# Output blocks of the end in the load buffers, and their stores as single 128-row transfers

## The chip, the cores and the metric

The kernel runs on one core of a Trainium2 chip. The time is the device time of one execution in microseconds (us). A core has TensorE (PE, matrix products into PSUM), VectorE (DVE), ScalarE (ACT), GpSimd (POOL) and SyncE (SP, which in this kernel only issues transfers), and 16 DMA engines that move data between the core's on-chip memory and DRAM. A transfer is issued by an instruction on SP or ACT; each of the two has its own DMA queue (q1 is SP's, q10 is ACT's in the profile).

## The reference

Eight batches of sigmoid attention with 12 heads, 448 tokens and a head dimension of 64, then a mixing layer over the tokens:

```python
scores = q @ k.T / sqrt(64) - log(448)
x = concat_heads(sigmoid(scores) @ v)          # 8 x 448 x 768
W_tok = (x @ w_q) @ (x @ w_k).T / sqrt(64)     # 448 x 448 per batch
out = relu(W_tok @ x) @ w_out                  # 8 x 448 x 768, float32
```

The output is 8 x 448 rows of 768 floats, 11 MB in all. A row is 3072 bytes.

## The kernel before, in words

All instructions are emitted in an order written out by hand: the string `PLAN` (L126) holds one letter per step, and the loop at L801 emits each. `S` and `P` are attention steps, `W`, `N`, `U`, `M` those of the mixing layer, and `O`/`o`/`I`/`i` a part of the last product (`relu(...) @ w_out`); a small letter puts its PSUM copy on ACT, a capital one on DVE. The string ends `...IxiiNIIuiIMiImmIIIOooOOOOoOOoooooo`.

The tokens of a batch are numbered `t = 7 p + i` with p of 0..63 and i of 0..6. Two batches form a pair `w`; its 14 values of (batch, i) are taken two at a time, in seven chunks `m` = 0..6. A chunk is 128 output rows: 64 tokens of one i on partitions 0 to 63 and 64 tokens of the next on partitions 64 to 127, each with 768 columns, computed as two halves of 384 columns (`nb` 0 and 1). The output of a chunk is 384 KB. Rows of one i lie 7 x 3072 bytes apart in DRAM; rows of i and i+1 of the same p are neighbours.

The last pair (w = 3) is what the change touches. Its chunks 0 to 2 are computed by `out_halves` (L535): for each of the two i values, two groups of 64-row products, an ACT or DVE copy (L557), and a DVE addition (L558); then two stores of 64 x 2 x 384 floats on SP (L567). Its chunks 3 to 6 are computed by `out_chunk` (L576) after everything else: 12 matmuls a chunk at L595, a copy out of PSUM per half (L624), and the function `store` (L600). In chunk 6 the second half is cut in two again, DVE copies one piece (L621) and ACT the other (L622), and each half of 384 columns is stored by itself. `store` issues one transfer for each 64 partitions: the first on SP, the second on ACT where `tail` is true, which it is for chunks 3 to 6 of the last pair (the attention is done by then).

The finished block lies in a tile `o`. These come from a pool of three buffers (`p_o`, L60), taken in turn, for all output of the kernel; a buffer can be written again once the stores that read it have landed. The inputs come through six other buffers of 128 x 896 floats (`lds`, L103), also taken in turn, by `ld_next` (L106). The last load is issued at 138.8 us of the span. The set `cast` holds all loads that have been converted; it has `len(ORDER) + 2` members when none is outstanding.

Of the kernel before, what the change touches and what calls it, by code (L numbers as in the profile page):

```python
# [9 lines left out]
F32 = mybir.dt.float32  # L10
# [7 lines left out]
def kernel(  # L18
# [12 lines left out]
    nc = tc.nc  # L31
    B, H, S, HD = q.shape
    D = H * HD
    DH = moe_w_q.shape[1]
    assert DH == HD == 64 and S == 448 and D == 768
    P = 128
    NI, NP = 7, 64
    NU = B
    NJ = H // 4
    NC = D // P  # L40
    NB = D // 2
# [6 lines left out]
    def pool(name, bufs, **kw):  # L48
        return ctx.enter_context(tc.tile_pool(name=name, bufs=bufs, **kw))
# [10 lines left out]
    p_o = pool("o", 3)  # L60
# [10 lines left out]
    def bank2():  # L71
        n = free2.pop(0)
        return n, pairs[n], pairs16[n]

    def bank1():
        if halves:
            n, b = halves.pop(0)
        else:
            n, b = free2.pop(0), 0
            halves.append((n, 1))  # L80
        return (n, b), pairs[n][:, b], pairs16[n][:, b]

    def release(fb):
        if isinstance(fb, int):
            free2.append(fb)
        elif (fb[0], 1 - fb[1]) in halves:
            halves.remove((fb[0], 1 - fb[1]))
            free2.append(fb[0])
        else:
            halves.append(fb)  # L90
# [15 lines left out]
    def ld_next():  # L106
        nld[0] += 1
        return lds[(nld[0] - 1) % 6]
# [386 lines left out]
    ot = {}  # L495
# [39 lines left out]
    def out_halves(act):  # L535

        if opened:
            w, m, part, fb, ps = opened.pop()
        else:
            w, m, nb = chunks.pop(0)  # L540
            assert nb < 0
            part = 0
            ot[0] = p_o.tile([P, 2, NB], F32, tag="o", name="o")
        o = ot[0]
        b, h = divmod(part, 2)
        if not h:
            fb, ps, _ = bank2()
        for c in range(3 * h, 3 * h + 3):
            t0 = 2 * S * c + m * P + b * NP
            for y in range(2):  # L550
                for x in range(2):
                    nc.tensor.matmul(  # L552
                        ps[HALF[x], y, 0:NB], mxs[w][HALF[y], t0 : t0 + NP], wout16[HALF[y], c, x * NB : (x + 1) * NB],
                        start=(c == 0), stop=(c == NC - 1),
                    )
        if h:
            COPY["s" if act else "v"](out=o[:, b], in_=ps[:, 0, 0:NB])  # L557
            nc.vector.tensor_tensor(out=o[:, b], in0=ps[:, 1, 0:NB], in1=o[:, b], op=ALU.add)  # L558
            release(fb)
        if part < 3:  # L560
            opened.append((w, m, part + 1, fb, ps))
            return
        (b0, i0), (b1, i1) = divmod(2 * m, NI), divmod(2 * m + 1, NI)
        for x in range(2):
            cols = slice(x * NB, (x + 1) * NB)
            if b0 == b1:
                nc.sync.dma_start(  # L567
                    out=out[2 * w + b0].rearrange("(p i) d -> p i d", i=NI)[:, i0 : i1 + 1, cols], in_=o[HALF[x]],
                )
                continue  # L570
            for y, (b, i) in enumerate(((b0, i0), (b1, i1))):
                nc.sync.dma_start(
                    out=out[2 * w + b].rearrange("(p i) d -> p i d", i=NI)[:, i, cols], in_=o[HALF[x], y],
                )

    def out_chunk(act, tail):  # L576

        if opened:
            w, m, nb, fb, ps = opened.pop()
            part = 1  # L580
        else:
            w, m, nb = chunks.pop(0)
            if nb < 0:
                nb = 0
                chunks.insert(0, (w, m, 1))
            fb, ps, _ = bank2() if w == NU // 2 - 1 and not chunks else bank1()
            part = 0
        last = isinstance(fb, int)
        if nb == 0 and not part:
            ot[0] = p_o.tile([P, D], F32, tag="o", name="o")  # L590
        o = ot[0]

        def block(ps, w0, w1, c0, c1):
            for c in range(c0, c1):
                nc.tensor.matmul(  # L595
                    ps, mxs[w][:, 2 * S * c + m * P : 2 * S * c + (m + 1) * P],
                    wout16[:, c, w0:w1], start=(c == 0), stop=(c == NC - 1),
                )

        def store(cols):  # L600
            for y in range(2):
                b, i = divmod(2 * m + y, NI)
                eng = nc.scalar if tail and y else nc.sync
                eng.dma_start(
                    out=out[2 * w + b].rearrange("(p i) d -> p i d", i=NI)[:, i, cols],
                    in_=o[HALF[y], cols],
                )

        ps = ps if last or part else ps[:, 0:NB]
        if last:  # L610
            for c in range(part * NC // 2, (part + 1) * NC // 2):
                for x in range(2):
                    block(ps[:, x, 0 : NB // 2], NB + x * NB // 2, NB + (x + 1) * NB // 2, c, c + 1)
        else:
            block(ps, nb * NB, (nb + 1) * NB, part * NC // 2, (part + 1) * NC // 2)
        if not part:
            opened.append((w, m, nb, fb, ps))
            return
        if last:
            h = NB // 2  # L620
            nc.vector.tensor_copy(out=o[:, NB : NB + h], in_=ps[:, 0, 0:h])  # L621
            nc.scalar.copy(out=o[:, NB + h :], in_=ps[:, 1, 0:h])  # L622
        else:
            COPY["s" if act else "v"](out=o[:, nb * NB : (nb + 1) * NB], in_=ps)  # L624
        release(fb)
        split = tail and w == NU // 2 - 1 and m == NI - 1
        if nb or split:
            store(slice(nb * NB, (nb + 1) * NB) if split else slice(0, D))
# [23 lines left out]
    def cols(r):  # L652
        return slice(r.start * HD, r.stop * HD)
# [8 lines left out]
        out=ident, in_=ident, compare_op=ALU.not_equal, fill=1.0, base=0,  # L662
# [8 lines left out]
    for t in wqks:  # L671
# [3 lines left out]
    ORDER = (  # L675
# [5 lines left out]
    )  # L681
# [7 lines left out]
    ORDER = [(x[0], int(x[1:])) for x in ORDER.replace(".", "").lower().split()]  # L689
# [3 lines left out]
    used, loaded, cast = set(), set(), set()  # L693
# [72 lines left out]
    for t16, t32, r, e in (  # L766
# [3 lines left out]
            out=t16[:, r].rearrange("p i b d -> p b i d"),  # L770
            in_=t32[:, :, cols(r)].rearrange("p b (i d) -> p b i d", d=HD),
# [3 lines left out]
    def tr_part(nm, t16, r, e):  # L775
# [13 lines left out]
        out=k016[:, K3].rearrange("p i b d -> p b i d"), in_=k0[:, :, cols(K3)].rearrange("p b (i d) -> p b i d", d=HD),  # L789
# [11 lines left out]
    for t in PLAN:  # L801
# [6 lines left out]
        tail = done["S"] == N * NI  # L808
# [3 lines left out]
        elif kind == "P":  # L812
            n, i = divmod(c, NI)
# [25 lines left out]
        elif kind == "x":  # L839
            tr_x(c, tail, t in "XY", "s" if t in "yY" else "v")  # L840
        elif kind == "W":
            mlp_wqk(*divmod(c, NC), tail, t in "wl", t in "Ll")
        elif kind == "C":
            for y in range(2):
                nc.sync.dma_start(out=wout16[HALF[y], NC + c, :], in_=wout16[HALF[1 - y], c, :])
        elif kind == "N":
            mlp_wkn(c)
        elif kind == "U":
            (mlp_tmp_tiled if t in "Tt" else mlp_tmp)(c, t in "ut")
        elif kind == "M":  # L850
            u, x = divmod(c, NC // 2)
            mlp_mix(u, x, t == "m", tail)
            if x == NC // 2 - 1:
                if u // 2 in TW:
                    chunks.extend((u // 2, ((u % 2, i), (u % 2, 6 - i))) for i in range(3))
                    if u % 2:
                        chunks.append((u // 2, ((0, 3), (1, 3))))
                else:
                    chunks.extend((u // 2, m, -1) for m in (range(3, NI) if u % 2 else range(3)))
        elif kind == "O":  # L860
            if (opened or chunks)[0][0] in TW:
                out_pair(t == "o")
            elif t in "Ii":
                out_halves(t == "i")
            else:
                out_chunk(t == "o", tail)
# [29 lines left out]
```

## Time and profile before

| | us |
|---|---|
| median of 3 runs | 189.16 (188.65 to 190.88) |
| the profiled execution, its own time | 189.54 |
| its span, first to last instruction | 187.8 |
| PE busy | 176.3 (94%) |
| ACT busy | 163.6 (87%) |
| DVE busy | 140.8 (75%) |
| POOL busy | 106.7 (57%) |
| granted clock of PE | 0.999 |

The profile is of one execution, so its span is 1.74 us shorter than the same execution's own time, and that time is 0.38 us over the median. The span is followed by PE nearly from end to end; the shares of busy time say little on the last 10 us, in which PE ends its work and only copies and stores remain. This stretch is read from the timeline, the waits and the DMA view.

### The profile page before, as it was taken

To read this page: it belongs to the slowest core of one execution; us is meant where nothing else is said; L and a number is where in the kernel's file an instruction comes from. 1 tells how busy PE (TensorE), PEld (TensorE's weight loads), DVE (VectorE), ACT (ScalarE), POOL (GpSimd) and SP (SyncE) were. 2 spreads that over 40 slices of the span, in tenths; PEclk is the share of its full clock that TensorE was granted. 3 is DMA by queue.
4 is the path that set the end of the run, shared out by engine and by line. 5 is a ranking of instruction groups with operands and counts; after the bars stand their busy time and mean duration, and the time that the engine had idled before them with its cause. 6 is when DMAs were issued, how large, how long until landed. Compare 5 with 4: busy or idle time off the path is not lost.

```text
span 187.8 us, 8516 instructions
## 1 busy us (share of the span) xinstructions
PE 176.3 (94%) x3648; PEld 115.8 (62%) x3648; DVE 140.8 (75%) x216; ACT 163.6 (87%) x210; POOL 106.7 (57%) x145
## 2 busy tenths in 40 slices
PE   7898899989999999999999999999999999999990
PEld 7343456544555454565555776667998889776650
DVE  3534697677868999999898999888768565787810
ACT  4699999999999989999999999898999989975130
POOL 1457796972959989899899767495032910010000
PEclk9999999999999999999999999999999999999999
DMA  5999999954699989999988999993998733603485
GB/s 175 364 388 377 333 381 393 362 171 139 204 335 402 404 254 292 383 289 310 271 237 262 335 336 353 287 296 101 247 339 282 184 92 87 165 13 85 101 237 168
DMA packets 26389, 48.97 MB, mean 261 GB/s; under 512 B 4080, under 2 KB 20208, under 8 KB 26352
## 3 DMA queue, kind: packets, MB, share of 16 engines
q1 hardware_dynamic: 25952, 47.65, 78.1%
q10 hardware_dynamic: 400, 0.79, 1.2%
q8 instruction: 28, 0.46, 1.1%
q14 instruction: 9, 0.07, 0.1%
HBM read 35.78 MB, written 11.01 MB: 249 GB/s over the span
## 4 chain that ended last, share of the span: by engine, by line
PE 63%; DVE 14%; DMA 7%; POOL 5%; ACT 4%; issue 3%; ACTq 0%; DVEq 0%
PE banks L302 14%; PE banks L515 12%; PE banks L320 11%; PE banks L595 8%; DMA ld<-in_k_dram 4%; ACT at L307 4%; PE banks L552 3%; DMA ld<-in_v_dram 3%; DVE xt L329 3%; DVE qk L227 2%; PE banks L386 2%; POOL qk L187 2%; PE banks L668 2%; PE banks L343 2%; DVE mx L458 2%
## 5 line engine op out<-in xcount | busy, mean ns | idle before, releaser
L307 ACT ACTIVATE at<-banks 128x896 bf16<-128x896 f32 x168 | 141.6, 927 | 5.5 <-PE banks L302 4.4
L302 PE MATMUL banks<-qk 64*64 64x448 bf16 x672 | 63.6, 360 | 4.0 <-ACT at L307 1.1
L320 PE MATMUL banks<-at,v 64*64 64x448 bf16 x672 | 46.6, 350 | 0.2
L302 PEld LDWEIGHTS <-qk 64*64 64x64 bf16 x672 | 26.1, 105 | 27.2 <-issue 16.0
L515 PE MATMUL banks<-wout,mx 64*64 64x384 bf16 x672 | 35.3, 323 | 0.0
L187 POOL CAST qk<-ld 128x896 bf16<-128x896 f32 x24 | 28.6, 1205 | 7.7 <-DVE qk L258 4.3
L197 POOL CAST v<-ld 128x896 bf16<-128x896 f32 x22 | 20.4, 933 | 18.7 <-DMA ld<-in_v_dram 15.2
L320 PEld LDWEIGHTS <-v 64*64 64x64 bf16 x672 | 23.1, 106 | 7.8 <-issue 1.7
L515 PEld LDWEIGHTS <-mx 64*64 64x64 bf16 x672 | 24.4, 107 | 3.4
L329 DVE CAST xt<-banks 128x896 bf16<-128x896 f32 x20 | 21.6, 1083 | 4.9 <-ACT at L307 2.3
L458 DVE TENSOR_SCALAR mx<-banks 128x1024 bf16<-128x1024 f32 (+2 forms) x21 | 21.1, 1010 | 5.5 <-PE banks L482 3.3
L595 PE MATMUL banks<-wout,mx 128*128 128x384 bf16 (+1 forms) x138 | 24.7, 320 | 0.0
L595 PEld LDWEIGHTS <-mx 128*128 128x128 bf16 x138 | 11.9, 98 | 10.3 <-issue 4.5
L258 DVE STREAM_TRANSPOSE qk<-qk 128x448 f32<-128x448 f32 x24 | 14.9, 628 | 0.0
L395 POOL COPY wq<-wqk 64x448 bf16<-64x448 bf16 x6 | 3.7, 620 | 17.6 <-DVE wqk L394 17.3
L162 POOL COPY qk<-swap 32x448 uint32<-32x448 uint32 x20 | 11.8, 589 | 1.2
L524 DVE COPY o<-banks 128x768 f32<-128x768 f32 x9 | 8.6, 952 | 4.9 <-PE banks L515 4.2
L156 POOL COPY swap<-qk 32x448 uint32<-32x448 uint32 x20 | 11.1, 556 | 1.8 <-DVE qk L187 0.7
L159 POOL COPY qk<-qk 32x448 uint32<-32x448 uint32 x20 | 11.1, 556 | 1.2
L624 ACT COPY o<-banks 128x384 f32<-128x384 f32 x10 | 4.8, 485 | 7.1 <-PE banks L595 4.9
L227 DVE STREAM_TRANSPOSE qk<-qk 32x448 f32<-32x448 f32 x16 | 10.2, 636 | 0.4
L386 PE MATMUL banks<-xt,wqk 64*64 64x448 bf16 x144 | 9.9, 350 | 0.0
(91 smaller groups left out, 220.8 us busy)
## 6 DMA issues: line engine op xcount, KB each, us to landing
ld<-in_q_dram SPq DMA_DIRECT2D x24, 448.0 KB, 6.4
ld<-in_v_dram SPq DMA_DIRECT2D x24, 448.0 KB, 6.6
ld<-in_k_dram SPq DMA_DIRECT2D x23, 448.0 KB, 6.0
out_dram<-o SPq DMA_DIRECT2D x51, 192.0 KB, 3.8
ld<-in_moe_w_out_dram SPq DMA_DIRECT2D x6, 384.0 KB, 4.4
wout<-wout SPq DMA_DIRECT2D x12, 96.0 KB, 6.2
out_dram<-o ACTq DMA_DIRECT2D x3, 192.0 KB, 3.3
qk<-mv SPq DMA_DIRECT2D x8, 56.0 KB, 2.2
```

The source lines that it names most:

```text
L187: COPY[e](out=f[:, :, "qk".index(nm)].rearrange("p e i d y -> p e y i d"), in_=ld.pop((nm, n)).rearrange("p (y i e d) -> p e y i d", y=2, ...
L197: COPY[e](out=t16.rearrange("p i b d -> p b i d"), in_=ld.pop((nm, n)).rearrange("p b (i d) -> p b i d", i=NI),)
L227: nc.vector.transpose(out=qk[n][other : other + 32, h].rearrange("p t i n -> p (t i n)").bitcast(F32), in_=w[own : own + 32, 1 - h],)
L258: nc.vector.transpose(out=qk[n][:, t].rearrange("p t i n -> p (t i n)").bitcast(F32), in_=w)
L302: nc.tensor.matmul(sc[HALF[h], g, 0:S], qk[n][HALF[g], h, 1, i, :], qk[n][HALF[g], h, 0].rearrange("p i n -> p (i n)"), start=True, stop=True,
L307: nc.scalar.activation(at, sc[:, :, 0:S], ACTF.Sigmoid, bias=attn_bias, scale=attn_scale)
L320: nc.tensor.matmul(ps[HALF[g], h, 0:S], ld["v16", n][HALF[h], i, g, :], ats[n, i][HALF[h], g, :], start=(i == 0), stop=(i == NI - 1),)
L329: COPY[eng](out=xt(u, j)[:, :, 0:S], in_=ps[:, :, 0:S])
L386: nc.tensor.matmul(ps[HALF[x], y, 0:S], wqk16[HALF[y], c, 64 * x : 64 * x + 64], xt(u, c // 2)[HALF[y], c % 2, 0:S], start=(c == 0), stop= ...
L458: nc.vector.tensor_scalar(dst, ps, moe_scale, 0.0, ALU.mult, ALU.max)
L515: nc.tensor.matmul(ps[HALF[x], y, 0:NB], mx[HALF[y], u, b, 64 * (i - 3 * y) : 64 * (i - 3 * y) + 64], wout16[HALF[y], slot(y, b), x * NB : ...
L595: nc.tensor.matmul(ps, mxs[w][:, 2 * S * c + m * P : 2 * S * c + (m + 1) * P], wout16[:, c, w0:w1], start=(c == 0), stop=(c == NC - 1),)
```

## The change

Three edits, all for the last pair of batches.

1. In `out_halves` the block is a piece of the next load buffer in turn, once all loads have been converted. In `out_chunk` the same holds for the last pair. In the built program, chunks 0 to 6 take the load buffers 1, 2, 3, 4, 5, 0 and 1 in this order. The pool of three output buffers stays for all other blocks.
2. `store` issues everything on SP's queue.
3. Where `tail` is true and both i values of the chunk are of the same batch (chunks 4, 5 and 6; chunk 3 has i = 6 of one batch and i = 0 of the next), `store` issues one transfer of 128 rows in place of two of 64.

In the built program, the instruction of such a transfer has 128 rows of 768 (or 384) floats on the on-chip side, and on the DRAM side 2 x 64 rows of 768 (or 384), the 2 being the outermost count. The old stores have 64 rows on both sides. Nothing else changes in any engine's order.

```diff
@@ out_halves
-            ot[0] = p_o.tile([P, 2, NB], F32, tag="o", name="o")
+            ot[0] = (
+                ld_next()[:, 0:D].rearrange("p (b x) -> p b x", b=2) if len(cast) == len(ORDER) + 2
+                else p_o.tile([P, 2, NB], F32, tag="o", name="o")
+            )
@@ out_chunk
         if nb == 0 and not part:
-            ot[0] = p_o.tile([P, D], F32, tag="o", name="o")
+            late = w == NU // 2 - 1 and len(cast) == len(ORDER) + 2
+            ot[0] = ld_next()[:, 0:D] if late else p_o.tile([P, D], F32, tag="o", name="o")
@@ store
         def store(cols):
+            b, i = divmod(2 * m, NI)
+            if tail and i + 1 < NI:
+                nc.sync.dma_start(
+                    out=out[2 * w + b].rearrange("(p i) d -> i p d", i=NI)[i : i + 2, :, cols],
+                    in_=o[:, cols],
+                )
+                return
             for y in range(2):
                 b, i = divmod(2 * m + y, NI)
-                eng = nc.scalar if tail and y else nc.sync
-                eng.dma_start(
+                nc.sync.dma_start(
                     out=out[2 * w + b].rearrange("(p i) d -> p i d", i=NI)[:, i, cols],
                     in_=o[HALF[y], cols],
                 )
```

## The prediction

> **What bounds the kernel now.** I read the chain that ended last first, to see what the change can reach. Cut to the last 20 us, it is PE without a gap up to 182.57, and then ACT alone (start, duration, what):
>
> ```profile
> 174.71 7.85 PE banks L595 x53
> 182.57 0.02 issue
> 182.59 0.49 ACT o L624
> 183.08 0.02 issue
> 183.10 0.50 ACTq L604
> 183.59 0.04 issue
> 183.64 0.32 ACT o L622
> ```
>
> So an ACT copy, an ACT transfer issue and an ACT copy stand one behind the other once PE is done, and then the last stores. Next the list of waits from 168 us on, for what held the copies (engine, line, releaser: total, times, longest):
>
> ```profile
> DVE o L624 <- DMA out_dram<-o: 3.0, 1, 3.0
> ACT o L624 <- DMA out_dram<-o: 2.1, 1, 2.1
> ```
>
> Both are chunk 5, which waits for the buffer of chunk 2 until 181.3. Then ACT's timeline:
>
> ```profile
> 178.76 0.48 ACT L624 COPY o<-banks 128x384 f32<-128x384 f32 x1 [2.45 <-PE banks L595]
> 179.26 0.50 ACTq L604 DMA_DIRECT2D out_dram<-o  x1
> 181.37 0.48 ACT L624 COPY o<-banks 128x384 f32<-128x384 f32 x1 [2.14 <-DMA out_dram<-o]
> 181.99 0.48 ACTq L604 DMA_DIRECT2D out_dram<-o  x1
> 182.59 0.48 ACT L624 COPY o<-banks 128x384 f32<-128x384 f32 x1 [0.73 <-PE banks L595]
> 183.10 0.50 ACTq L604 DMA_DIRECT2D out_dram<-o  x1
> 183.64 0.32 ACT L622 COPY o<-banks 128x192 f32<-128x192 f32 x1 [0.57 <-ACT o L624]
> 183.99 0.50 ACTq L604 DMA_DIRECT2D out_dram<-o  x1
> ```
>
> Chunk 6's first half (182.59) was late behind chunk 5 and its issue, not behind PE. Last, the transfers. In stretches (PE, PEld, DVE, ACT, POOL busy, clock, DMA share, GB/s):
>
> ```profile
> 60.00:64.00 4.00, 3.97 (x63) 1.95 (x52) 3.88 (x7) 4.00 (x6) 3.70 (x7) 1.00 1.04 404
> 178.50:179.00 0.50, 0.50 (x5) 0.29 (x3) 0.00 (x0) 0.24 (x1) 0.00 (x0) 1.00 0.98 184
> 181.00:181.50 0.50, 0.50 (x5) 0.31 (x4) 0.16 (x1) 0.13 (x1) 0.00 (x0) 1.00 1.00 393
> ```
>
> and the packets of 174 us to the end, and then of the whole span:
>
> ```profile
> DMA packets 1386, 2.38 MB, mean 159 GB/s; under 512 B 225, under 2 KB 1001, under 8 KB 1385
> ...
> DMA packets 26389, 48.97 MB, mean 261 GB/s; under 512 B 4080, under 2 KB 20208, under 8 KB 26352
> ```
>
> The small packets count engines. From 174 us, 14 stores are issued (4 of L567, 10 of L604), and 14 x 16 = 224 of the 225. Over the span the list of issues has 159 transfers: 159 x 16 = 2544, and the two loads of w_q and w_k have 2 x 128 x 6 = 1536 rows of 256 bytes; 2544 + 1536 = 4080, exactly. So each transfer leaves one small packet on each engine that it uses, and **every transfer of before uses all 16**. Their outermost counts are 128, 64 or 32 rows, on both sides.
>
> **Part 1, the buffers.** A block in a load buffer waits for nothing: the loads ended long ago, and chunk 6, which takes chunk 0's buffer again, waits for stores issued at 170.7. The copies then follow PE. Those of chunk 3 and 4 came at 175.83, 176.81, 177.78 and 178.76, 0.98 apart; so chunk 5's come at 179.74 (DVE) and 180.72 (ACT), and chunk 6's first half at 181.70 instead of 182.59. Its last pieces come when PE ends, 182.64 (DVE's time now). PE gains nothing: it was busy for 2.00 of 2.00 us in both 178 to 180 and 180 to 182. Adding: the last data is ready at 182.64 + 0.36 = 183.00 instead of 183.64 + 0.32 = 183.96, a gain of 0.96 us.
>
> **Part 2, one queue.** ACT loses five issues of 0.48 to 0.57 us; the one at 183.10 is in the chain and already in the 0.96. SP is busy with L567 until 178.04. Then come two stores of chunk 3 (0.59 to 1.02 each, L604's rows), so it is free for chunk 4 at 179.4 to 180.0, where the data is ready at 179.24; I take 179.7. For chunk 5 (181.20) and 6 (182.18, 183.00) an issue of under 1 us is in time. No engine but SP is queued behind these.
>
> **Part 3, one transfer of 128 rows.** This decides. The new transfer has 128 rows on chip and 2 x 64 in DRAM. No row of before shows an outermost count that isn't a multiple of 16. To share a transfer, each engine must be given a piece of both sides; if they are cut along their outermost counts, 64 = 16 x 4 gives 16 pieces, as the small packets show, while 128 against 2 can be cut alike only in **two**. If the rows are dealt out one after another, it is still 16.
>
> I take two. They would be the same two each time (the first ones), and so one queue of bytes: chunk 4, 5 and 6 are 3 x 393,216 bytes, half of it on each engine, 589,824 bytes. The pace of one engine from three rows: 404 / 16 = 25.3 GB/s (loads, all engines at work); 393 / 16 = 24.6 (stores). The row of 184 GB/s is left out as a pace: there, too, the share is 0.98, but both halves of the partitions weren't in flight. The nearest for engines that never run out of work is the first: 589,824 / 25.3 = 23.3 us. Slow end: from 178.0 to 182.3 chunks 2 to 4 (1.18 MB) went at 274 GB/s, 17.1 per engine, 34.5 us. Fast end: the best short slice of a store from 170 to 174, 471 GB/s, 29.4 per engine, 20.1 us.
>
> The start: chunk 5's old store was issued at 181.96 and its bytes flowed from 183.0, 1.0 later; chunk 4's would flow from 179.7 + 1.0 = 180.7. End of data 180.7 + 23.3 = 204.0. In before the last packets are at 186.2 and the span ends at 187.8, 1.6 later: 205.6. Against 187.8 this is **+17.8 us**, with the gain of part 1 lost in it, since the copies wait for no store any more. The profiled execution would be 189.54 + 17.8 = 207.3, and on the median of the runs 189.16 + 17.8 = **207.0 us**. The ends: 203.8 and 218.2.
>
> The Trainium skill, DMA: Bandwidth & Descriptors, in the section on why a DMA increments its semaphore by 16 and not by 1, says that the number of engines is the largest up to 16 that divides the slowest count of both sides, and that the lowest-numbered ones are taken. By it these stores get engines 0 and 1; that all of before's have 16 agrees with the count of small packets, and no run yet shows a 2. Its Specifications give about 27 GiB/s to an engine; an estimate by that is 20.3 us, or 204.0 on the median.
>
> **Rivals.** *All 16 engines, not slower.* The rows are dealt one by one. Then the last store is issued at 183.0 instead of 183.98, and 192 KB in one transfer lands in 2.7 to 2.8 us (the median of that size from 174 us on) where the old pieces took 2.5 and 2.9: -0.98 with up to 0.2 lost, say -0.8: 188.4, within 2%. For it: merging was harmless for 128-row loads, of which 16 engines carry each. Against: those have 128 outermost on both sides. It decides if the small packets stay at 16 a transfer. The Trainium skill's Rules for kernel authors on the same page advise one 128-partition transfer in place of two halves, by which this rival would hold; the rows of 184 and 393 GB/s only show that one half alone is slow.
>
> *Two engines, but another two for each transfer.* Then they overlap. Chunk 5, ready at 181.2, flows from 182.2 for 196,608 / 25.3 = 7.8 us, to 190.0; chunk 6's second half (98,304 bytes each, 3.9 us) from 184.0 to 187.9. The span ends at 190.0 + 1.6 = 191.6, +3.8: 193.0. Nothing in the rows speaks for a choice that moves on.
>
> *The buffers still wait.* If chunk 6 waited on its load buffer, the last copy would be where it is now: 189.2, if all engines are used. The stores of chunk 0 land 2.7 to 4.2 us after 170.7 to 171.9, five us too early for that.
>
> **How the numbers follow.** Two engines 0.85, all 16 engines 0.09, changing pairs 0.04, buffers that wait 0.02. The range is that of the first case, 203.8 to 218.2; with some 0.95 of its chance inside, it holds 0.81. About 2% is what a measurement of this kernel can tell from no change: under 185.4 or over 192.9. Slower: 0.85 + half of 0.04 = 0.87; within: 0.09 + 0.02 + 0.02 = 0.13, of which 0.01 for a gain over 2% that no sum gives.
>
> **What would show it.** Part 1: no wait of L624 for a store, ACT's last copy done by 183.0. Part 2: no issue on ACT, no packets on q10. Part 3: with two engines, small packets over the span are 151 x 16 + 4 x 2 + 1536 = 3960 (with 16 it is 155 x 16 + 1536 = 4016), and after 183 us the DMA share stays at 2/16, about 0.12, with some 50 GB/s for 20 us in which no engine computes. 4016, a share near 1.0 at the end and a span under 188 would make the prediction wrong.

## The result

The changed kernel takes 208.47 us (median of 6 runs, 207.12 to 210.55) against 189.09 us for the kernel before: 1.098 times as long, with a 95% interval of 1.093 to 1.104. The ratios here and below leave out runs that lie over 1.5% above the fastest run of the same kernel (here the one of 210.55), while the medians are of all runs. Forecast were 207.0 us and a range of 203.8 to 218.2.

The profiled execution took 208.04 us, with a span of 205.9. The copies first, which the change was to free. ACT's timeline of the changed kernel from 174 us to its end:

```profile
174.99 0.48 ACT L634 COPY ld<-banks 128x384 f32<-128x384 f32 x1 [1.84 <-PE banks L599]
177.91 0.48 ACT L634 COPY ld<-banks 128x384 f32<-128x384 f32 x1 [2.44 <-PE banks L599]
179.86 0.48 ACT L634 COPY ld<-banks 128x384 f32<-128x384 f32 x1 [1.47 <-PE banks L599]
180.79 0.48 ACT L634 COPY ld<-banks 128x384 f32<-128x384 f32 x1 [0.45 <-PE banks L599]
181.78 0.32 ACT L632 COPY ld<-banks 128x192 f32<-128x192 f32 x1 [0.51 <-PE banks L599]
```

No copy waits for a store, no transfer is issued on ACT, and ACT's last copy ends at 182.10. The last DVE copy begins at 181.76 here and at 182.64 before: PE ended 0.88 us earlier in this execution. This is no effect of the change. ACT's last instruction ahead of the first copy of the last pair (L373) already begins 0.93 us earlier here, at 166.86 instead of 167.79, and the end of PE's work lies at 182.09 and 183.76 in two executions of one kernel below. What is left of the difference comes after that point: 24.1 us to the end of the span instead of 5.2. The waits from 168 us on (engine, line, releaser: total, times, longest), and SP's:

```profile
ACT ld L634 <- PE banks L599: 6.2, 4, 2.4
...
DVE ld L634 <- PE banks L599: 1.8, 2, 1.4
```

```profile
SPq L901 <- DMA out_dram<-ld: 11.0, 1, 11.0
```

The two waits of 3.0 and 2.1 us for a store are gone, and one of 11.0 us stands at SP's very end, for the last store. Why it takes so long is seen in the stretches of the changed kernel (PE, PEld, DVE, ACT, POOL busy, granted clock, DMA share, GB/s):

```profile
180.00:181.00 1.00, 1.00 (x10) 0.74 (x9) 0.00 (x0) 0.55 (x2) 0.00 (x0) 1.00 0.36 108
181.00:182.00 1.00, 0.75 (x10) 0.52 (x7) 0.24 (x1) 0.49 (x2) 0.00 (x0) 1.00 0.09 22
182.00:183.00 1.00, 0.00 (x0) 0.00 (x0) 0.12 (x1) 0.10 (x1) 0.00 (x0) 1.00 0.12 37
183.00:184.00 1.00, 0.00 (x0) 0.00 (x0) 0.00 (x0) 0.00 (x0) 0.00 (x0) 1.00 0.13 52
...
190.00:195.00 5.00, 0.00 (x0) 0.00 (x0) 0.00 (x0) 0.00 (x0) 0.00 (x0) 0.50 0.13 52
...
200.00:203.00 3.00, 0.00 (x0) 0.00 (x0) 0.00 (x0) 0.00 (x0) 0.00 (x0) 0.50 0.13 50
```

A DMA share of 0.13 is 2 engines of 16. They are busy from 182 until the data ends near 204.4, 22 us, and move 50 to 52 GB/s in all from 183 on. And the packets of the whole span:

```profile
DMA packets 26269, 48.97 MB, mean 238 GB/s; under 512 B 3960, under 2 KB 20088, under 8 KB 26232
```

The 3960 small packets are 151 transfers with 16, four with 2, and the 1536 short rows of the weights.

### The profile page after: what moved, and what is told of

Read it like the earlier page. It is cut to its first block, busy times and chain, and to the rows that moved or that the text cites. A ratio compares the mean times of both kernels' runs of the same rounds, so it can differ in the third digit from the quotient of the medians.

```text
span 205.9 us, 8496 instructions
## 1 busy us (share of the span) xinstructions
PE 175.7 (85%) x3646; PEld 115.8 (56%) x3648; DVE 140.0 (68%) x216; ACT 163.5 (79%) x210; POOL 107.3 (52%) x145
## 2 busy tenths in 40 slices
DMA packets 26269, 48.97 MB, mean 238 GB/s; under 512 B 3960, under 2 KB 20088, under 8 KB 26232
## 4 chain that ended last, share of the span: by engine, by line
PE 57%; ACT 14%; DVE 9%; issue 5%; DMA 3%; ACTq 0%; DVEq 0%
ACT at L307 14%; PE banks L302 11%; PE banks L515 11%; PE banks L320 10%; PE banks L599 10%; DMA ld<-in_k_dram 3%; PE banks L555 3%; DVE qk L227 3%; PE banks L386 2%; PE banks L430 2%; PE banks L360 2%; PE banks L678 2%; DVE mx L458 2%; DVE xt L329 1%; PE banks L343 1%
## 5 line engine op out<-in xcount | busy, mean ns | idle before, releaser
L515 PEld LDWEIGHTS <-mx 64*64 64x64 bf16 x672 | 24.2, 107 | 3.5
L162 POOL COPY qk<-swap 32x448 uint32<-32x448 uint32 x20 | 12.4, 621 | 1.2
L373 DVE COPY xn<-banks 128x1024 bf16<-128x1024 bf16 (+1 forms) x13 | 8.2, 628 | 2.5 <-PE banks L360 2.4
```

Of the source, the lines that this page charges most:

```text
L515: nc.tensor.matmul(ps[HALF[x], y, 0:NB], mx[HALF[y], u, b, 64 * (i - 3 * y) : 64 * (i - 3 * y) + 64], wout16[HALF[y], slot(y, b), x * NB : ...
```

## The experiments

The time after PE's end is given with each, from the start of the last DVE copy to the end of the span, since PE's end moves from one execution to the next. It is 5.16 us before and 24.14 after.

### One part at a time

**Part 1 alone**, the load buffers:

```diff
--- changed kernel
-            b, i = divmod(2 * m, NI)
-            if tail and i + 1 < NI:
-                ...  # the 128-row store
-                return
             for y in range(2):
                 b, i = divmod(2 * m + y, NI)
-                nc.sync.dma_start(
+                eng = nc.scalar if tail and y else nc.sync
+                eng.dma_start(
```

> Part 1 of the change alone: late blocks in the load buffers, old stores of 64 rows on SP and ACT. Theory (two engines for a 2 x 64 row transfer are the whole loss): all stores run on 16 engines, so no loss; chunk 5 and 6 are copied as PE ends them, the last store is issued at about 183.1 instead of 183.98 on the scale of the kernel before, so 188.2 (0.9 under the kernel before), 4080 small packets. Rival (stores out of the load buffers are the slow ones): about 208.

188.43 us, 0.9960 of the kernel before (0.9936 to 0.9984), 4.38 us after PE's end instead of 5.16, 4080 small packets. The gain is there, 0.6 us of the 0.9 that were expected. The load buffers are not what costs the 19 us.

Part of what is missing lies outside the span. The time of an execution less its span is 1.74 to 1.85 us in every run of the kernel before, and 2.10 to 2.20 us in every run of the kernels with the load buffers: this one, the changed kernel and all others below that have them. In the one kernel below that has the 128-row stores and the old buffers it is 1.79. So some 0.35 us comes with part 1; no run tells why.

**Parts 1 and 2**, the 128-row branch taken out and all stores left on SP:

```diff
--- changed kernel
-            b, i = divmod(2 * m, NI)
-            if tail and i + 1 < NI:
-                ...
-                return
```

> Parts 1 and 2: load buffers, all stores on SP's queue, still 64 rows each. Theory of two engines: 16 engines, no loss; against e1 the second of the last two stores is issued behind the first on SP, 0.47 later: 188.2 to 188.7, 4080 small packets. Rival (one queue can't carry the stores of the end): about 208, with a low DMA share to the end.

189.55 us, 0.9995 of the kernel before (0.9965 to 1.0025), 4.78 us after PE's end, 4080 small packets. One queue carries the stores of the end, but the gain of part 1 is not seen any more. The interval overlaps with that of part 1 alone, so the difference between the two is not sure. SP's timeline of this kernel shows what one queue costs:

```profile
178.08 6.83 SPq L607 DMA_DIRECT2D out_dram<-ld  x10
```

Ten issues one behind the other take until 184.91, and the last of them begins at 184.3, while the last copies end by 183.0: SP itself is late, by 1.3 us. Of this, 0.4 us shows after PE's end (4.78 against 4.38 us), near the 0.47 expected.

**Parts 2 and 3 without part 1**, the three old output buffers kept:

```diff
--- changed kernel
-            late = w == NU // 2 - 1 and len(cast) == len(ORDER) + 2
-            ot[0] = ld_next()[:, 0:D] if late else p_o.tile([P, D], F32, tag="o", name="o")
+            ot[0] = p_o.tile([P, D], F32, tag="o", name="o")
...  # the same in out_halves
```

> Parts 2 and 3 without part 1: the three output buffers as before, the 128-row stores on SP with 2 outermost. Theory of two engines: the copies come up to 0.96 later, but the two engines work through the same 589,824 bytes each from chunk 4 on, so the time is that of the changed kernel, 207 to 209, with 3960 small packets, a DMA share of 0.13 to the end. Rival (load buffers and merged stores are both needed for the loss): 189.

208.69 us in a single run, 24.2 us after PE's end, 3960 small packets. So the whole loss comes with the 128-row stores, and part 1 is worth nothing beside it, as the prediction had it.

### The order of the DRAM side

One thing differs from the changed kernel, the order of the counts on the DRAM side:

```diff
--- changed kernel
-                    out=out[2 * w + b].rearrange("(p i) d -> i p d", i=NI)[i : i + 2, :, cols],
+                    out=out[2 * w + b].rearrange("(p i) d -> p i d", i=NI)[:, i : i + 2, cols],
```

> The changed kernel with one difference: the DRAM side of a 128-row store is 64 x 2 x 768 instead of 2 x 64 x 768, the same bytes to the same region in the same number of transfers. The 128 rows of chunks 4 to 6 land in another order, so the output is a permutation there. Theory of two engines, by the outermost count: 64 gives 16 engines, 4016 small packets, 188.2 to 188.6. Rival (128 rows in one transfer, or a store in one piece, is slow whatever its order): 207 to 208.

188.46 us, 0.9958 of the kernel before (0.9926 to 0.9991), 3.75 us after PE's end. Its packets, and its SP timeline:

```profile
DMA packets 26325, 48.97 MB, mean 264 GB/s; under 512 B 4016, under 2 KB 20144, under 8 KB 26288
```

```profile
178.60 4.21 SPq L607 DMA_DIRECT2D out_dram<-ld  x4
```

4016 is 155 transfers with 16 engines each. The same number of transfers, queue, buffers and bytes: with 64 outermost instead of 2, 20 us are gone. Four issues are done by 182.81, where the 64-row stores needed ten and were late.

This order does not write the rows to their places, since the 128 partitions hold all 64 values of p for one i and then all 64 for the next. To use it, the rows of a chunk would have to be computed in (p, i) pairs; that was not tried on the chip.

### Which engines

Chunk 5 goes to ACT's queue:

```diff
--- changed kernel
-                nc.sync.dma_start(
+                eng = nc.scalar if m == 5 else nc.sync
+                eng.dma_start(
                     out=out[2 * w + b].rearrange("(p i) d -> i p d", i=NI)[i : i + 2, :, cols],
```

> The changed kernel with chunk 5's 128-row store issued on ACT's queue, the others on SP's. If the same two engines are taken whatever the queue: the DMA share at the end stays at 0.13, some 51 GB/s, and the time stays at 207 to 209. If the limit is the queue (a queue hands one transfer to two engines at a time) or each transfer gets other engines: two transfers overlap, share 0.25 and 100 GB/s for some 8 us, 8 us less: about 200.

207.8 us in a single run. Stretches of this kernel:

```profile
186.00:190.00 4.00, 0.00 (x0) 0.00 (x0) 0.00 (x0) 0.00 (x0) 0.00 (x0) 0.50 0.13 52
190.00:195.00 5.00, 0.00 (x0) 0.00 (x0) 0.00 (x0) 0.00 (x0) 0.00 (x0) 0.50 0.13 51
195.00:200.00 5.00, 0.00 (x0) 0.00 (x0) 0.00 (x0) 0.00 (x0) 0.00 (x0) 0.50 0.13 51
```

and its queues from 186 to 188 (packets, MB, share of 16 engines):

```profile
q10 hardware_dynamic: 18, 0.06, 6.8%
q1 hardware_dynamic: 16, 0.05, 6.0%
```

Two queues, and still two engines at work. Other engines for each transfer, or a limit of the queue, would have shown 0.25. Nor does one transfer wait for the other: both queues move bytes in the same 2 us, each with about the time of one engine (1/16 is 6.25%), so the two transfers share the two engines.

### Is it the shape or the number?

No 128-row store here; each 64-row store is cut in 62 rows and 2:

```diff
--- parts 1 and 2
-                nc.sync.dma_start(
-                    out=out[2 * w + b].rearrange("(p i) d -> p i d", i=NI)[:, i, cols],
-                    in_=o[HALF[y], cols],
-                )
+                for r in (slice(0, 62), slice(62, 64)) if tail and m > 3 else (slice(0, 64),):
+                    nc.sync.dma_start(
+                        out=out[2 * w + b].rearrange("(p i) d -> p i d", i=NI)[r, i, cols],
+                        in_=o[64 * y + r.start : 64 * y + r.stop, cols],
+                    )
```

> No merged store: each 64-row store of chunks 4 to 6 is made as one of 62 rows and one of 2 rows, all on SP, load buffers kept. The number of engines by the largest divisor up to 16 of the outermost count: 62 gives 2 and 2 gives 2, so nearly the same bytes on the same two engines as in the changed kernel, 206 to 210, and 2 small packets a store: 149 x 16 + 16 x 2 + 1536 = 3952 (chunk 4 and 5 four stores each, chunk 6 eight). By the smaller of the count and 16: 62 rows on 16 engines, and about 190, with eight of these stores at 16 and eight at 2, 4064. If only the order 2 x 64 is at fault: 190.

209.77 us in a single run, 26.4 us after PE's end. The packets:

```profile
DMA packets 26293, 48.97 MB, mean 236 GB/s; under 512 B 3984, under 2 KB 20112, under 8 KB 26256
```

The counts in the expectation were miscounted by two full transfers: it is 151 x 16 + 16 x 2 + 1536 = 3984 with 2 engines for 62 rows, and 4096 with 16 for them. The run shows 3984. So a plain store of 62 rows, with the same count on both sides, also gets two engines: neither the 2 x 64 order nor a count under 16 is needed. The largest divisor of 62 up to 16 is 2, as the first of the three expectations has it. It is also the largest power of two that divides 62, and the counts of all runs here (128, 64, 32, 62 and 2) don't tell these two rules apart.

### The price of one such store

Chunk 4 alone stored as 2 x 64 rows, or the second half of chunk 6 alone, the rest as 64-row stores on SP:

```diff
--- changed kernel
-            if tail and i + 1 < NI:
+            if tail and m == 4:                        # or: m == 6 and cols.start == NB
```

> Only chunk 4 is stored as 2 x 64 rows; chunk 3, 5 and 6 as 64-row stores on SP, load buffers kept. Same two engines: each of them has 196,608 bytes of chunk 4 and 1/16 of chunks 5 and 6 behind it, 49,152 bytes, 245,760 in all, 9.7 us at 25.3 GB/s from 180.7: end of data 190.4, span 4.2 over the kernel before, 193.3. If a store that is issued later passes it on these engines, or engines are others each time: data ends at 188.5, span +2.3, 191.4. If the loss were a fixed cost of a merged store, a quarter of 19.4: 194.

> Only the second half of chunk 6 is stored as 2 x 64 rows of 384, everything else as 64-row stores on SP, load buffers kept. Theory of two engines, cost by bytes: 98,304 bytes on each, 3.9 us from 184.0: 187.9, span +1.7, 190.8. A fixed cost of a merged store, a quarter of 19.4 us: 194. No cost where nothing is queued behind it: 188.4.

A single run of each gave 196.4 and 194.34, both above what the bytes give, and the second on the rival of a fixed cost. But PE had ended late in both, at 183.15 and 183.76. So both were run four times more, together with a kernel that issues chunk 4 as two stores of half the columns:

```diff
--- chunk 4 alone
+                for part in (slice(0, NB), slice(NB, D)):
                     nc.sync.dma_start(
-                        ...[i : i + 2, :, cols], in_=o[:, cols],
+                        ...[i : i + 2, :, part], in_=o[:, part],
```

> Chunk 4 alone as one store of 2 x 64 rows again, now with repeats, since one look moves by up to 1 us with the end of PE. Two engines, bytes and a slow start of 1 to 2 us as the looks showed: 194.5 to 196. By bytes at the full pace alone: 193.3. Fixed cost a store: 194, and then e9 4.9 above this.

> The second half of chunk 6 alone as one store of 2 x 64 rows of 384, now with repeats. Bytes and a slow start: 192 to 193.5. By bytes at the full pace alone: 190.8. Fixed cost a store: 194, the same as for chunk 4's store of four times... of twice the bytes.

> Chunk 4 alone as 2 x 64 rows, as two stores of 384 columns in place of one of 768: the same bytes on the two engines, twice the stores. The one look at the single store gave 196.4. Theory of two engines with the cost in the bytes: within 1 us of the single store. Fixed cost for each such store (4.9 us, a quarter of 19.4): 4.9 over the single store, 201.

| 2 x 64 stores | us, median | ratio to before (95%) |
|---|---|---|
| chunk 6's second half, 98,304 bytes an engine | 192.71 | 1.018 (1.013 to 1.022) |
| chunk 4, 196,608 bytes an engine | 195.51 | 1.032 (1.027 to 1.036) |
| chunk 4 in two stores | 196.34 | 1.037 (1.031 to 1.043) |

Twice the stores for the same bytes is 0.8 us, not 4.9: there is no large fixed cost. The bytes alone explain neither: both are about 2 us over the forecast by bytes, 190.8 and 193.3. For chunk 6, two causes are in the rows. The first is the pace at the start. Stretches of the kernel with chunk 6's second half alone:

```profile
184.00:185.00 1.00, 0.00 (x0) 0.00 (x0) 0.00 (x0) 0.00 (x0) 0.00 (x0) 1.00 0.29 80
185.00:186.00 1.00, 0.00 (x0) 0.00 (x0) 0.00 (x0) 0.00 (x0) 0.00 (x0) 0.78 0.13 32
186.00:187.00 1.00, 0.00 (x0) 0.00 (x0) 0.00 (x0) 0.00 (x0) 0.00 (x0) 0.50 0.13 38
187.00:188.00 1.00, 0.00 (x0) 0.00 (x0) 0.00 (x0) 0.00 (x0) 0.00 (x0) 0.50 0.13 49
188.00:189.00 1.00, 0.00 (x0) 0.00 (x0) 0.00 (x0) 0.00 (x0) 0.00 (x0) 0.50 0.13 51
```

Both engines are busy, but from 185 to 187 they move 32 and 38 GB/s and only then 50: (51 - 32) / 51 + (51 - 38) / 51 = 0.6 us. The other is SP. Its timeline in the same execution:

```profile
177.54 5.55 SPq L614 DMA_DIRECT2D out_dram<-ld  x8
183.20 0.64 SPq L607 DMA_DIRECT2D out_dram<-ld  x1
```

Eight 64-row issues hold SP until 183.09, so the last store is issued at 183.20, while its data was ready at 182.45 (DVE's last copy ends then): 0.75 us. That is the lateness of parts 1 and 2 again. Of the remaining half microsecond, 0.35 is what the load buffers add outside the span. The 2.2 us of chunk 4, whose store is issued in time, are not taken apart beyond these 0.35.

## Why the prediction was right

- **Part 3, two engines.** Shown: 3960 small packets as forecast, a share of 0.13, and the loss disappears when 64 stands outermost. The Trainium skill's rule (DMA: Bandwidth & Descriptors, the section on why a DMA increments its semaphore by 16 and not by 1) of the largest divisor up to 16 of both slowest counts agrees with all runs: 16 for 64 against 128, 2 for 2 against 128, and 2 for 62 against 62. The largest power of two would agree as well.
- **The same two each time.** Shown by chunk 5 on the other queue, where both queues together keep two engines busy. The rival of changing pairs falls.
- **The pace.** 25.3 GB/s for an engine was taken from the loads. The rows give 50 to 52 GB/s for two, 25 to 26 each. The two ends of the range (17.1 and 29.4) were far off. The Trainium skill's about 27 GiB/s (DMA: Bandwidth & Descriptors, Specifications), which is 29 GB/s, is above what these rows show.
- **The start and the end.** Data was forecast to end 21.4 us after the last DVE copy begins (204.0 against 182.64). It ended near 204.4, which is 22.6 after 181.76; of these 1.2 us, the two microseconds from 181 to 183 at 22 and 37 GB/s make (52 - 22) / 52 + (52 - 37) / 52 = 0.9. The sum has no term for such a slow start. From there to the end of the span it was 1.5 us instead of 1.6.
- **The sum.** The span is 205.9 against 205.6, closer than it deserves: PE's early end hides 0.9 us of the slow start. The time around the span was taken over from the kernel before, 1.74 us, and was 2.1, as in all kernels with the load buffers. These two make 0.3 and 0.4 of the 1.5 us between 207.0 and 208.47. The other 0.8 lies between a profiled execution and the median: in the kernel before it was 0.38 over its median, here 0.43 under it. That the forecast came so near is in part luck.
- **Part 1.** The copies follow PE as forecast: the last data is ready 0.36 us after PE's end instead of 1.32, 0.96 earlier. For the buffers alone 0.9 was forecast and 0.6 measured (0.4%, with an interval of 0.2 to 0.6%), and the 0.35 us outside the span is a term that the sum did not have.
- **Part 2.** "An issue of under 1 us is in time" failed, without effect on the time. In the changed kernel the issues of the 128-row stores are held while the two engines are at work:

```profile
L607 SPq DMA_DIRECT2D out_dram<-ld x4: 547/2928/7237, 178.5 to 186.6; - x4
```

  Minimum, median and maximum are in ns: the last of the four began at 186.6 and took 7.2 us, though its data was there at 182.1. The engines never ran dry by that, so it cost nothing here. With 64-row stores it does cost: with SP's ten issues the gain of part 1 is not seen any more.
- **The rival of 16 engines** fell for this order of the counts, and its time of 188.4 is what the order with 64 outermost takes (188.46). No run here makes loads in halves, so that merging was harmless for the loads isn't shown; what is shown is that 128-row loads get 16 engines.

The kernel with part 1 alone takes 188.43 us, 0.4% less than the kernel before; no kernel here that writes every row to its place is faster.

## What to carry to other kernels

Before two stores are merged into one, look at the outermost count of both sides as the instruction carries it: if 16 doesn't divide both, the transfer runs on fewer engines, by the rule that all runs here agree with; here it was 2 of 16 at 51 GB/s, and each later transfer of that kind queues behind it on the same ones. The profile shows it without a guess: where the rows are longer than 512 bytes, count the packets under 512 bytes per transfer, and look for a DMA share that stands still at a few sixteenths, here 2/16. A store in the middle of a kernel may hide this, which no run here tried; at the end, where nothing is left to cover it, every byte is paid.

## What was not expected of the hardware

- A transfer on two engines begins slowly. In the kernel with chunk 6's second half alone both engines are busy from 185 to 187 and move 32 and 38 GB/s, and 49 to 51 from then on. In the changed kernel it is 22 and 37 GB/s from 181 to 183, with shares of 0.09 and 0.12, so there the engines also stood idle in part, and 50 to 52 from then on. Busy engines at a low pace are not peculiar to two engines. The kernel before, with all 16, has them as chunk 5's first store begins:

```profile
183.00:184.00 1.00, 0.00 (x0) 0.00 (x0) 0.00 (x1) 0.39 (x2) 0.00 (x0) 1.00 0.99 194
```

  This is 12 GB/s for each busy engine; in the next microsecond it is 295 GB/s at a share of 0.86, 21 an engine. The prediction puts such rows down to one half of the partitions being in flight alone; whether that bears on the stores on two engines, or what else slows their start, no run here tells.
- The issuing instruction on SP was held for up to 7.2 us while two engines were at work, where a 64-row store takes about 0.6. What stands behind it on SP's queue waits too: the fourth 128-row store was issued 4.5 us after its data was there (186.6 against 182.1).
- When PE has no work, its granted clock in these rows falls from 1.00 to 0.50, but not after a fixed time. In the changed kernel, whose PE ends at 181.76, it is 1.00 from 183 to 184, 0.75 in the next microsecond and 0.50 from 185 on; in the kernel with part 1 alone, whose PE ends at 181.62, it is still 1.00 from 185 to 186. The mean clock of 0.948 of this run is that idle tail, and no slower matmul.
